# A fused attention, gated MLP and rational MLP in fp32: attention tiles of 64 queries by 96 keys with two heads on 128 partitions, in place of 96 by 128 of one head

## The chip, the cores and the metric

The kernel runs on one core of one Trainium2 chip. The metric is the device time of one launch in microseconds (us), as the median of several runs. Five engines work beside each other: TensorE (PE: matmuls and transposes; PEld is its loading of weights), VectorE (DVE), ScalarE (ACT), GpSimd (POOL) and SyncE (SP, which here issues the DMAs).

## The reference, cut to what matters

```python
def _attn_ref(q, k, v):                     # (4, 8, 576, 64) fp32
    window, dilation = 32, 4
    scores = (1.0 / np.sqrt(D)) * np.matmul(q, k.transpose(0, 1, 3, 2))
    rel = pos[:, None] - pos[None, :]
    mask_plain = (rel >= 0) & (rel < window)
    mask_dil = (rel >= 0) & (rel < window * dilation) & (rel % dilation == 0)
    masks = [mask_plain if h < H // 2 else mask_dil for h in range(H)]
    scores = np.where(masks[None], scores, -1e9)
    scores = scores - np.max(scores, axis=-1, keepdims=True)
    attn = np.exp(scores)
    attn = attn / (np.sum(attn, axis=-1, keepdims=True) + 1e-09)
    return np.matmul(attn, v)

x = attn_out.transpose(0, 2, 1, 3).reshape(2304, 512)
x = ((x @ w1) * (x @ w2) @ w3) @ w_out       # 512 -> 1024 -> 1024 -> 512
h = x @ w_in                                 # 512 -> 2048
P = a[0] + a[1] * h + a[2] * h * h + a[3] * h * h * h
Q = 1.0 + np.abs(b[0]) * np.abs(h) + np.abs(b[1]) * h * h
return (P / (Q + 1e-06)) @ moe2_w_out        # 2048 -> 512
```

The weights of the two MLPs arrive as fp64, and the kernel turns their words into fp32 itself.

## The kernel before

**Two phases.** `phase1` does the attention, the product of `w3` and `w_out` (so that the first MLP has one matrix less), the first MLP, and the decoding of all fp64 weights. `phase2` does the second MLP, `step(i)` by `step(i)`, with matmuls in `hmm` (L867) and `l4` (L917). The change doesn't touch `phase2`.

**Attention.** A unit `u` is one batch and one pair of heads (16 units), and a half unit `G` is half of its queries (32 of them). The queries of a dilated head are sorted by their position modulo 4, so that both masks become a band of 32 keys and a tile of queries needs one short piece of the keys. A tile is 96 queries by 128 keys, three tiles per head and half. The steps of a half unit are:

- Q, `att_qk` (L362): for each tile and head a matmul of K = 64, with the queries as weights (64 x 96) and 128 columns of keys moving. The two heads lie on partitions 0 to 63 and 64 to 127 and write to two banks of PSUM. An fp32 matmul is two records in the trace.
- `att_mask` (L382, DVE): adds the mask, scales, and takes the row's minimum; six per half. `att_exp` (L390, ACT): exponential and row sum; six per half. `att_sums` (L395, L397) and `att_norm` (L402), DVE.
- T, `att_pt` (L409): a transpose on PE for each tile and head, 96 x 128 of the probabilities as weights and 96 columns of the identity moving; three per head. `att_pc` (L415, ACT) copies the result out of PSUM.
- V, `att_pv` (L424): for each tile and head a matmul with 128 x 64 of the values as weights and 96 columns moving; the two heads write to partitions 0 to 63 and 64 to 127 of one bank.
- `att_high` (L464, ACT) and `att_low` (L468, DVE) split the result in a high and a low part for the MLP.

**The MLP and the weights.** `w3_mm` (L480) multiplies `w3` by `w_out`; `l1` (L501) and `l2` (L533) are the first MLP, 12 matmuls of 128 x 512 per output tile. `load` issues the DMA of a slab of weights; `scale` (L231) and `top_bits` (L262) on ACT and `ends` (L267) and `middle` (L271) on DVE decode it. The first slabs (`CUTS`) come in two pieces. `warm_up` (L318) fills PE with 11 matmuls before the first Q and 14 behind it.

**The order.** `phase1` makes a list of jobs, each with an engine, what it must come after and which buffers it takes, and `Plan.order` issues them in the order that the table `ORDER` gives, three hexadecimal digits a job. Each engine's queue then follows that order, and the waits between engines come from semaphores. `att_runs` groups Q and V: the first eight half units run one by one, later ones in pairs (V of two half units, then Q of the next two).

Of the kernel before, what the change touches and what calls it, by code (L numbers as in the profile page):

```python
# [41 lines left out]
QT = 96  # L42
# [20 lines left out]
CUT_W3 = (5, 6, 7)  # L63
BY_ACT1, BY_ACT2 = 0, 16
# [5 lines left out]
RUN_FROM = 8  # L70

# [12 lines left out]
def q_bank(g):  # L84
    return ("sc", "px")[g == 1 or g >= RUN_FROM and g % 2]


def t_bank(g):
    return ("px", "sc")[g >= RUN_FROM and g % 2 == 0]


def v_bank(g):
    return "sc" if g >= 30 else ("px", "acc")[g >= RUN_FROM]
# [6 lines left out]
    "1e70000011eb1f11e81e91f52001fb1ea1ef1ed1ec00300f0041f31f22051ee1f00061f71f60050101f41f81f91fa007"  # L100
    "20201120327c27b2010082042061fd1fc20701c52320a00201b20f1fe1ff21901227e00900a20820c21420b00b00d27d"
    "2b920d20e20901300c21100e22301401501701e21021e21b21221321a22a01802a21c21d21621523803a01f021217218"
    "02001622522422602b22703b23102221f22027f28028222c01d02302402524622b28122802601901a22122d22e02c027"
    "22222f22923a23902823f2c003c24d28423023b02d02e03802923323203d23c02f23423524825225705a05923d236030"
    "04903903e24903f24124704124004023703123e28328528628703203304a03403628824a24224303503724b04204304b"
    "24424c24525c2ab26125925804504624f24e28904404c04728a28b04828d04d25028c2512542532c228f29104f26605c"
    "28e25525625a25b27426d2932952972902c329205705805d25e2ad06826325d04e06925f05e050294296051264260053"
    "29805205529926726826926a2ac2620602652ae2af26f27005f06127626e05427127706329a2f82e32ce07e05b2d507f"
    "2b22dc2b005606a26b2722732752bb2ba06b06d07629b06229c26c06c06e2782b106429e07706f07107006629d2d62c1"
    "0650722c42bc2792d70672d82bd29f07307807427a2a02de2b42c50750792b307b2b52d92c62da2dd2a107a2b607c2b7"  # L110
    "2a22db07d2b82df30646330d2c70802ea0812f10b70990b609831409a2ff2a32a52a72a82a92be2aa08d08e2c82c92e5"
    "08f2ca31b0822bf2cb0832a42e031d09009109346409246508431c31e3210940962cc2cf2cd2a62d00852ec2e1086087"
    "0882e232332208908b32730830f0950972eb08a08c2e62d12d23242ed2ee2d32e42ef2fa2f33292d42e72f046646709b"
    "09c09d0b231f0f40d44694682e809e2f90b43102fb3280a732a2fc0b32e90a832d09f0a932f0a00a20b50aa0a132e333"
    "2f246a3003010ab0ac0ad46b3300ae0b00a30a50af3350b10a42fd0a63340b93022f43202f52f62fe46c3032f746d331"
    "32530730e3040d03360ba0c50c630930a30546e46f0d50b83390bc3163320bb33a33b30b0c70bd0c830c33c0be0c00d1"
    "0bf3110c933f34033d4703370ca0cb4713413120d20ce0c30c10cc3130d34724734753450cd0cf0c20c4315317318326"
    "31932b34231a3380d70d80ee0f00ef0f14763430da34747747847932c0d93460f21113480e333e0db0e53490dc3440dd"
    "0e40e634a0de0e70e834b34c34d34e3520ea0e10df0e90f30d647b47c47d47e47f47a1104814740ec0eb34f3530ed0e0"
    "0e23563503543553510f510110248248348448548012f48748610c1030f635735835910d10e1041051060f835a35d108"  # L120
    "0f710710a10f0f935b35e3614880fa0fc0fb35f0ff0fd48948a48b1090fe36310010b36211336411f11436012e36748d"
    "48e36935c48f49049149312a12112c11636812036a11512211736d36f36e37049449549649737337412312412511811a"
    "11911d12812611b37537612b12d37911c11e12736536637712937b36b49213011214c13149918937149a49b49c49d49f"
    "48c14d49e14837213213337a37c14914a13437f13513d13f38113e1401361381373804a03823781414a14a24a313b385"
    "38613938714314214b14414613a13c14538314738b38836c14f4a516c4a63894984a74a84a94ab18816b14e4a4166167"
    "37d16816938d38c15038e38f15215115b15c37e3841531544ac15e15d4ad4ae4af38a39015f1601551561614b14aa16a"
    "39139239339416216339539639715739816415816515939c15a39939a4b216d4b34b44b539d16e16f1841861791704b7"
    "1c539b1a64b618a17139e17a18717217318517417c17b1751764b817d17f17e39f1771781821803a31811834b94ba4bb"
    "18b3a03a43a13a54bd4b03a73a218c18d19719852418e3a94be3a83ad18f3aa3af1a21994bf4c04c11a81c43a64bc1a7"
    "4c31903ae3b01921913b31951933b419a19b19c19d3b11941963b51a419e3b23b61a51a31a03b919f1a14c43bb3b71a9"  # L130
    "4c54c64c74c91c01c23ba1b53b81b71b61c33bc1aa1ab1b83bf3c03c13bd1b93be3c24ca1ad4cb4cc4cd1ba1bb3c53c7"
    "3c63cb1ac1ae1af1bc1b11be4cf1b03cd3ab3ac1c13c81b33cc1bd1bf1b21b41c73c94d03ce4d14d24d33ca1c81de3c3"
    "1e01c64d54c84ce1df1e11ca3d13d33d21c93d43c41d33d53cf1d43d63d04d61d51d64d74d84d91d71d81cb1d91cc4db"
    "4da4c23d73d83d93da3de3e21da1ce1cd1dc1d11cf1db1dd1d01d23e34dc1e24dd4de4df1e31e54e11e41e63e43e53e6"
    "3e73e93ea3eb3e84d44e04e24e34e44e53ec4e73ed3ef3ee3df3f03f33f54e83f43e03f64e94ea4eb4ed3e14e63f73f1"
    "3f93fb3fa3fc3ff4014ee4ef4f04f14004023fd4033db3f23fe4044054064073dc3f84084f34f44f54f64f74f84f94f2"
    "40b40d40c40e41140f4094134124144fa4104fb4fc4fd4ff41741841940a5254fe52641a41b41541641c500501502503"
    "5054ec50650750850950b50450a3dd50c50d50e50f51141d41e41f42042142442842242542642742342942a42b42f433"
    "43443543643943b42c42d43a43c51242e51351451543043f44143d43e44044244544743751651751051851951a51b51d"
    "44644843144b44c43251c44944d44344443844e51e51f52052152252852e45145345245445745945845a45d45e45544f"  # L140
    "44a45052945f52a45b52f46046153046245645c52752b52c53153253352d"
# [45 lines left out]
class Kern:  # L187
# [91 lines left out]
    def high_g(self, s):  # L279
        s["w"] = self.gp.tile([P, 2, TB], F32R, tag="g", bufs=8, name="wg")  # L280
        self.nc.scalar.copy(s["w"][:, 0], s["x"])
# [10 lines left out]
    def consts(self, pool):  # L292
        nc = self.nc

        nc.scalar.preload_act_table_set("natural_log_exp_and_others")
        self.ident = pool.tile([P, P], F32, name="ident")
        nc.gpsimd.memset(self.ident, 0.0)
        nc.gpsimd.affine_select(out=self.ident, in_=self.ident, compare_op=ALU.not_equal,
                                fill=1.0, base=0, pattern=[[-1, P]], channel_multiplier=1)

        self.masks = pool.tile([QT, 3, P], F32, name="masks")
        nc.gpsimd.memset(self.masks, 0.0)
        for i in range(3):
            mk = self.masks[:, i]
            nc.gpsimd.affine_select(out=mk, in_=mk, compare_op=ALU.is_gt, fill=NEG, base=0,
                                    pattern=[[1, P]], channel_multiplier=-1)
            nc.gpsimd.affine_select(out=mk, in_=mk, compare_op=ALU.is_ge, fill=NEG, base=WIN,
                                    pattern=[[-1, P]], channel_multiplier=1)
        nc.gpsimd.memset(self.masks[:, 0, 0:WIN], NEG)
        mk = self.masks[:, 1, 0:80]  # L310
        nc.gpsimd.affine_select(out=mk, in_=mk, compare_op=ALU.is_gt, fill=NEG, base=48,
                                pattern=[[0, 80]], channel_multiplier=-1)
# [36 lines left out]
    def att_load_v(self, u):  # L349
        b, hp = divmod(u, HP)  # L350
        self.vb[u] = self.at.tile([P, 2, NTILE, D], F32, tag="vb", bufs=2, name="vb")
# [18 lines left out]
    def att_mask(self, G, h):  # L370
# [4 lines left out]
        if h == 0:  # L375
            self.pr[G] = at.tile([QT, 6, P], F32, tag="pr", bufs=3, name="pr")
            self.sm[G] = at.tile([QT, 3, 6], F32, tag="sm", bufs=4, name="sm")
        pr, sm = self.pr[G], self.sm[G]
        for t in range(3):
            mk = t if dil else (0 if half == 0 and t == 0 else 2)  # L380
            i = h * 3 + t
            nc.vector.tensor_tensor_reduce(  # L382
                out=pr[:, i], in0=self.sc[G][h][0:QT, t * P:(t + 1) * P], in1=self.masks[:, mk],
# [3 lines left out]
    def att_exp(self, G, h):  # L387
        pr, sm = self.pr[G], self.sm[G]
        for i in range(3 * h, 3 * h + 3):
# [711 lines left out]
```

## Time and profile before

| | |
|---|---|
| median of three runs | 824.01 us (823.68, 824.01, 827.56) |
| the profiled execution, its own time | 824.62 us |
| its span, first to last instruction | 822.8 us |
| PE busy | 814.1 us, 99% |
| PEld, DVE, ACT, POOL busy | 81%, 73%, 67%, 27% |
| the chain that ended last | PE 96%, DMA 2%, ACT 1%, DVE 1% |

The profile is of one execution. Busy time counts an engine's instructions; ends of matmuls are modelled, so that a matmul's duration overlaps the next one, and what a block of matmuls costs is read from its start to the start of the next block. L12 is line 12 of the kernel before. A row of the timeline gives start, length, engine, line, output and inputs, weights and moving shape, and the count; behind it in brackets the idle time before it.

### The profile page before, as it was taken

The page shows a single profiled execution, that of the slowest core. Times are in us where ns is not written, and L with a number is a line of the kernel's source. Part 1 is how long each engine was busy: PE and PEld are TensorE (multiplying, and loading weights), DVE is VectorE, ACT ScalarE, POOL GpSimd, SP SyncE. Part 2 cuts the span into 40 slices and gives each one's busy share as a digit, 9 for nine tenths or more (in the row PEclk, how much of TensorE's full clock was granted, in tenths as well). Part 3 has the DMA queues.
Part 4 walks back from the last instruction along what each step waited for, and adds up shares of the span by engine and source line. Part 5 has one row for each costly group of instructions (what it writes and reads, how often), then busy time and mean ns, then how long its engine had stood idle before and what let it go on. Part 6 is the DMA issues. An engine that isn't in the chain of part 4 may idle for free.

```text
span 822.8 us, 12622 instructions
## 1 busy us (share of the span) xinstructions
PE 814.1 (99%) x4426; PEld 668.8 (81%) x4426; DVE 602.7 (73%) x1325; ACT 547.5 (67%) x1223; POOL 225.2 (27%) x185
## 2 busy tenths in 40 slices
PE   8999999999999999999999999999999999999998
PEld 5556888888889988888888888888888888888886
DVE  6999999647777844325447888887789777797775
ACT  6999987555557632222438887777778777777773
POOL 1000000000000000000015655655547555465442
PEclk9999999999999999999999999999999999999999
DMA  8969434553456343544640000110001001001112
GB/s 302 363 229 362 137 120 135 167 183 108 145 192 204 105 146 115 192 141 140 235 136 25 27 14 14 28 37 14 14 14 38 27 14 25 2 25 53 51 52 77
DMA packets 38559, 90.74 MB, mean 110 GB/s; under 512 B 4192, under 2 KB 6240, under 8 KB 38496
## 3 DMA queue, kind: packets, MB, share of 16 engines
q1 hardware_dynamic: 38496, 89.93, 32.8%
q8 instruction: 35, 0.57, 0.3%
q14 instruction: 28, 0.23, 0.1%
HBM read 69.47 MB, written 20.45 MB: 109 GB/s over the span
## 4 chain that ended last, share of the span: by engine, by line
PE 96%; DMA 2%; ACT 1%; DVE 1%; issue 0%; SPq 0%; DVEq 0%
PE ab L501 24%; PE px L867 12%; PE ab L867 12%; PE acc L917 12%; PE sc L917 12%; PE acc L533 6%; PE ab L533 3%; PE sc L533 3%; PE acc L480 2%; PE ab L480 2%; PE sc L362 2%; PE acc L424 2%; PE px L409 1%; DMA words<-moe_w_out 1%; PE px L362 1%; PE sc L409 1%
## 5 line engine op out<-in xcount | busy, mean ns | idle before, releaser
L878 POOL TENSOR_TENSOR y<-y,v 128x512 f32<-128x512 f32 x72 | 96.4, 1339 | 551.9 <-DMA c<-wd 404.6
L501 PE MATMUL ab<-xs,w 128*128 128x512 f32 (+1 forms) x960 | 203.7, 371 | 0.2 <-DVE x2l L548 0.2
L501 PEld LDWEIGHTS ab<-xs,w 128*128 128x128 f32 x960 | 166.2, 189 | 31.0 <-DVE x2l L548 0.4
L917 PE MATMUL acc<-w,gg 128*128 128x512 f32 x432 | 109.1, 389 | 0.0
L917 PE MATMUL sc<-w,gg 128*128 128x512 f32 x432 | 108.9, 389 | 0.0
L867 PE MATMUL ab<-XS,w 128*128 128x512 f32 (+1 forms) x480 | 104.4, 368 | 0.0
L867 PE MATMUL px<-XS,w 128*128 128x512 f32 (+1 forms) x480 | 104.2, 368 | 0.0
L904 POOL TENSOR_TENSOR gg<-t,gg 128x512 fp32r<-128x512 f32 x72 | 94.1, 1307 | 10.8 <-ACT gg L903 10.1
L867 PEld LDWEIGHTS px<-XS,w 128*128 128x128 f32 x480 | 84.1, 188 | 15.3
L867 PEld LDWEIGHTS ab<-XS,w 128*128 128x128 f32 x480 | 84.1, 188 | 15.3
L917 PEld LDWEIGHTS acc<-w,gg 128*128 128x128 f32 x432 | 80.8, 188 | 16.6
L917 PEld LDWEIGHTS sc<-w,gg 128*128 128x128 f32 x432 | 80.8, 188 | 16.6
L390 ACT ACTIVATE pr<-pr,sm 96x128 f32<-96x128 f32 x192 | 74.9, 397 | 10.5 <-DVE sm L382 10.5
L895 DVE SCALAR_TENSOR_TENSOR v<-y,cs,r 128x512 f32<-128x512 f32 x72 | 71.0, 986 | 0.0
L231 ACT ACTIVATE dec<-words 128x512 f32<-128x512 f32 (+1 forms) x74 | 48.7, 665 | 27.9 <-DMA words<-moe_w_out 10.9
L513 DVE TENSOR_TENSOR p<-a_sb,ab 128x512 f32<-128x512 f32 (+1 forms) x40 | 25.3, 632 | 55.2 <-PE ab L501 38.3
L508 ACT COPY a_sb<-ab 128x512 f32<-128x512 f32 (+1 forms) x40 | 21.8, 546 | 61.2 <-PE ab L501 61.1
L887 ACT ACTIVATE r<-y,cs 128x512 f32<-128x512 f32 x72 | 52.1, 724 | 13.1 <-POOL y L878 12.8
L877 ACT ACTIVATE y<-v,cs 128x512 f32<-128x512 f32 x72 | 58.8, 817 | 2.4
L903 ACT CAST gg<-t 128x512 fp32r<-128x512 f32 x72 | 44.3, 615 | 15.1 <-DVE t L897 15.1
L533 PE MATMUL acc<-pp,w 128*128 128x512 f32 (+1 forms) x240 | 50.4, 368 | 0.0
L533 PEld LDWEIGHTS acc<-pp,w 128*128 128x128 f32 x240 | 41.8, 189 | 7.4
(107 smaller groups left out, 1241.2 us busy)
## 6 DMA issues: line engine op xcount, KB each, us to landing
words<-moe_w SPq DMA_DIRECT2D x31, 512.0 KB, 5.9
words<-moe_w_out SPq DMA_DIRECT2D x23, 512.0 KB, 4.2
words<-moe_w_in SPq DMA_DIRECT2D x16, 512.0 KB, 4.1
wd<-dec SPq DMA_DIRECT2D x32, 256.0 KB, 4.5
c<-wd SPq DMA_DIRECT2D x32, 256.0 KB, 2.7
vb<-v SPq DMA_DIRECT2D x16, 384.0 KB, 5.8
XS<-x2d SPq DMA_DIRECT2D x6, 1024.0 KB, 7.4
kT<-k SPq DMA_DIRECT2D x16, 304.0 KB, 4.8
```

The lines of the kernel that those rows point to most:

```text
L231: self.nc.scalar.activation(out=d.bitcast(F32), in_=s["words"].bitcast(F32)[:, :, 1], func=AF.Copy, scale=2.0 ** -112)
L390: self.nc.scalar.activation(out=pr[:, i], in_=pr[:, i], func=AF.Exp, scale=-1.0, bias=sm[:, 0, i:i + 1], accum_out=sm[:, 1, i:i + 1])
L501: self.nc.tensor.matmul(t[:, 0:nt], w[:, s[0], c * P:(c + 1) * P], xs[:, s[1], c], start=n == 0, stop=n == 11)
L533: self.nc.tensor.matmul(self.l2_acc[k, n][:, 0:nt], self.W3o[m][0][:, a, n * P:(n + 1) * P], self.p2[k, m][:, c, 0:nt], start=m == 0 and ( ...
L867: nc.tensor.matmul(t[:, e * nt:(e + 1) * nt], w[:, s[0], c * P:(c + 1) * P], XS[blk][:, s[1], c], start=n == 0, stop=n == 11)
L877: nc.scalar.activation(out=w, in_=v, func=AF.Identity, scale=self.b1, bias=self.b0)
L878: nc.gpsimd.tensor_tensor(out=w, in0=w, in1=v, op=ALU.mult)
L887: nc.scalar.activation(out=r, in_=yy[i][1], func=AF.Ln, bias=self.c1)
L895: nc.vector.scalar_tensor_tensor(out=v, in0=w, scalar=self.c1, in1=r, op0=ALU.add, op1=ALU.mult)
L903: nc.scalar.copy(t[:, 0], u)
L904: nc.gpsimd.tensor_tensor(out=t[:, 1], in0=u, in1=t[:, 0].bitcast(F32), op=ALU.subtract)
L917: nc.tensor.matmul(acc[g, blk][tk], t[:, s[0], j:j + P], w[:, s[1]], start=f + e == 0 and s == (0, 0), stop=f + e == FG - 1 and s == (1, 0))
```

## The change

It cuts the attention into nine tiles of 64 queries by 96 keys per unit (five in the first half, four in the second). The two heads of a pair stand on top of each other, on partitions 0 to 63 and 64 to 127, so that one mask, one exponential and one normalisation serve both. Q writes both heads to one bank (64 columns of weights each, 96 columns moving), T takes 64 x 96 of the probabilities with 64 columns of the identity moving and writes the heads to two banks, V has 96 x 64 as weights and 64 columns moving, of which the tile that lies across the middle is done in two parts of 32. The masks become six tiles of their own. T of a half unit is one job, no longer one per head. `ORDER` is another table.

```diff
-QT = 96
+QT = 64
+KW = 96
+TILES = ((0, 1, 2, 3, 4), (5, 6, 7, 8))
+PARTS = ((slice(0, 3), slice(3, 5)), (slice(0, 2), slice(2, 4)))
...
-    "1e70000011eb1f11e81e91f52001fb1ea1ef1ed1ec00300f0041f31f22051ee1f00061f71f60050101f41f81f91fa007"
+    "1c71cb1d10001d50011e01c91c81d31cd1d21cc1db1d71d61e501a1ca1d41cf1d91ce1d000300e1d81da1e20041ea1e1"
...
 def att_qk(self, G):
-        sc = self.sc[G] = [self.bank(q_bank(G)) for _ in range(2)]
-        for t in range(3):
-            j = (3 * half + t) * QT
+        sc = self.sc[G] = self.bank("sc")
+        for i, t in enumerate(TILES[half]):
             for h in range(2):
-                self.nc.tensor.matmul(sc[h][0:QT, t * P:(t + 1) * P],
-                                      qT[h * D:(h + 1) * D, j:j + QT],
-                                      kT[h * D:(h + 1) * D, j:j + P], start=True, stop=True)
+                r = slice(h * D, (h + 1) * D)
+                self.nc.tensor.matmul(sc[r, i * KW:(i + 1) * KW], qT[r, t * QT:(t + 1) * QT],
+                                      kT[r, t * QT:t * QT + KW], start=True, stop=True)
...
 def att_exp(self, G, h):
-        for i in range(3 * h, 3 * h + 3):
+        for i in range(5)[PARTS[G % 2][h]]:
...
-    def att_pt(self, G, h):
+    def att_pt(self, G):
-        pt = self.pt[G, h] = self.bank(t_bank(G))
-        for t in range(3):
-            self.nc.tensor.transpose(pt[:, t * QT:(t + 1) * QT], self.pr[G][:, h * 3 + t],
-                                     self.ident[0:QT, 0:QT])
+        pt = self.pt[G] = [self.bank("px") for _ in range(2)]
+        for i in range(len(TILES[G % 2])):
+            for h in range(2):
+                r = slice(h * QT, (h + 1) * QT)
+                self.nc.tensor.transpose(pt[h][0:KW, i * QT:(i + 1) * QT], self.pr[G][r, i], self.ident[r, r])
...
 def att_pv(self, G):
-        for t in range(3):
+        todo = ([(t, G, t, 0, QT if t < 4 else QT // 2) for t in range(5)] if half == 0 else
+                [(4, G - 1, 4, QT // 2, QT)] + [(t, G, t - 5, 0, QT) for t in range(5, 9)])
+        for t, g, i, a, b in todo:
+            at = t * QT + a - half * HS
             for h in range(2):
-                self.nc.tensor.matmul(xt[h * D:(h + 1) * D, t * QT:(t + 1) * QT],
-                                      vt[:, h, 3 * half + t], pT[:, h * 3 + t], start=True, stop=True)
+                self.nc.tensor.matmul(xt[h * D:(h + 1) * D, at:at + b - a],
+                                      vt[:, h, t], self.pT[g][:, h, i, a:b], start=True, stop=True)
```

The queue of PE where the pairs of half units have begun (`sc<-kT,qT` is Q, `px<-ident,pr` is T, `acc<-pT,vb` is V, `ab<-xs,w` is `l1`; the count is of matmuls, two trace records each for Q and V). Before:

```order
L362 MATMUL px<-kT,qT 96x128 x6
L501 MATMUL ab<-xs,w 128x512 x48
L409 MATMUL px<-ident,pr 128x96 x6
L409 MATMUL sc<-ident,pr 128x96 x6
L501 MATMUL ab<-xs,w 128x512 x12
L424 MATMUL acc<-pT,vb 64x96 x12
L362 MATMUL sc<-kT,qT 96x128 x6
```

and now:

```order
L366 MATMUL sc<-kT,qT 64x96 x18
L509 MATMUL ab<-xs,w 128x512 x36
L413 MATMUL px<-ident,pr 96x64 x8
L509 MATMUL ab<-xs,w 128x512 x12
L413 MATMUL px<-ident,pr 96x64 x10
L509 MATMUL ab<-xs,w 128x512 x12
L432 MATMUL acc<-pT,vb 64x64 x8
L432 MATMUL acc<-pT,vb 64x32 x4
L432 MATMUL acc<-pT,vb 64x64 x8
```

Twelve such rounds follow each other. Before, the transposes of the two half units stood together in six of the rounds and in two pieces in the other six; now they are in two pieces in all twelve, with `l1` or `l2` on both sides of each. Over the whole of phase 1, T is in 31 blocks before and in 32 now, and Q in 19 both times.

The queue of SP at the start of the program (`words` are weights, 256 KB where the shape is 128x512; `qT` 288 KB, `kT` 304 KB). Before:

```order
L213 DMA words<-moe_w_out 128x512
L342 DMA qT<-q 128x576
L347 DMA kT<-k 128x608
L213 DMA words<-moe_w_out 128x512
L213 DMA words<-moe_w 128x512 x2
```

and now:

```order
L209 DMA words<-moe_w_out 128x512 x2
L209 DMA words<-moe_w 128x512
L346 DMA qT<-q 128x576
L209 DMA words<-moe_w 128x512
L351 DMA kT<-k 128x608
```

The keys of the first unit were the third transfer and are now the sixth; the same six transfers come first both times. The queue of PE behind it still begins with 11 filler matmuls, the first Q (now 18 matmuls, before 12) and 14 filler matmuls.

## Rows read from the trace of the kernel before

**Rows 1.** The page, part 1: busy time, share of the span, instructions.

```profile
PE 814.1 (99%) x4426; PEld 668.8 (81%) x4426; DVE 602.7 (73%) x1325; ACT 547.5 (67%) x1223; POOL 225.2 (27%) x185
```

**Rows 2.** Windows: stretch, its length, then PE, PEld, DVE, ACT, POOL busy.

```profile
38.00:83.50 45.50, 45.49 (x264) 28.93 (x263) 44.42 (x128) 43.87 (x126) 0.00 (x0) 1.00 0.79 292
83.50:295.00 211.50, 211.31 (x1562) 181.06 (x1560) 164.48 (x583) 139.90 (x489) 0.00 (x0) 1.00 0.48 151
```

**Rows 3.** PE's waits, from the view of waits: total us, times, longest.

```profile
PE px L409 <- DVE pr L402: 1.7, 1, 1.7
...
PE px L424 <- ACT pT L415: 0.7, 1, 0.7
```

**Rows 4.** Timeline of PE, 91 to 114 us: one round and a half.

```profile
91.80 0.66 PE L409 MATMUL px<-ident,pr 96*128 96x96 f32 x6
92.24 3.00 PE L501 MATMUL ab<-xs,w 128*128 128x512 f32 x12
95.08 0.66 PE L409 MATMUL sc<-ident,pr 96*128 96x96 f32 x6
95.52 2.99 PE L501 MATMUL ab<-xs,w 128*128 128x512 f32 x12
98.44 1.21 PE L424 MATMUL acc<-pT,vb 128*64 128x96 f32 x24
99.58 0.90 PE L362 MATMUL sc<-kT,qT 64*96 64x128 f32 x12
100.31 0.82 PE L362 MATMUL px<-kT,qT 64*96 64x128 f32 x12
101.06 11.20 PE L501 MATMUL ab<-xs,w 128*128 128x512 f32 x48
112.09 0.66 PE L409 MATMUL px<-ident,pr 96*128 96x96 f32 x6
...
113.03 3.01 PE L501 MATMUL ab<-xs,w 128*128 128x512 f32 x12
```

**Rows 5.** Timeline of PE, 44 to 48.3 us, where half units run one by one.

```profile
44.61 0.72 PE L424 MATMUL px<-pT,vb 128*64 128x96 f32 x12
45.26 0.90 PE L362 MATMUL sc<-kT,qT 64*96 64x128 f32 x12
46.09 0.47 PE L409 MATMUL px<-ident,pr 96*128 96x96 f32 x3
...
48.09 0.41 PE L409 MATMUL px<-ident,pr 96*128 96x96 f32 x3
48.28 1.65 PE L480 MATMUL ab<-wg 128*128 128x512 f32 x6
```

**Rows 6.** Timeline of PE, 294 to 340 us: one long block and the next.

```profile
295.08 43.82 PE L501 MATMUL ab<-xs,w 128*128 128x512 f32 x192 [0.20 <-DVE x2l L548]
338.74 1.52 PE L533 MATMUL acc<-pp,w 128*128 128x512 f32 x6
```

**Rows 7.** Groups by form, PEld: weights' shape, count, busy us, mean ns.

```profile
L362 PEld LDWEIGHTS sc<-kT,qT 64*96 64x96 f32 x228 | 13.2, 159 | 3.0 <-issue 1.0
...
L424 PEld LDWEIGHTS acc<-pT,vb 128*64 128x64 f32 x264 | 11.3, 137 | 3.4 <-issue 2.1 <-ACT x L543 0.4 <-ACT dec L231 0.4
```

**Rows 8.** Timeline of PE and of SP's queue, first 12 us.

```profile
1.37 4.40 PE L318 MATMUL px<-ident 128*128 128x128 f32 x22 [1.37 <-POOL ident L298]
6.24 0.90 PE L362 MATMUL sc<-kT,qT 64*96 64x128 f32 x12 [0.47 <-DMA kT<-k]
...
7.73 3.39 PE L318 MATMUL ab<-ident 128*128 128x128 f32 x28
11.51 1.98 PE L480 MATMUL ab<-x 128*128 128x512 f32 x4 [0.39 <-DVE x L271]
...
2.59 1.38 SPq L213 DMA_DIRECT2D words<-moe_w  x3
```

**Rows 9.** DMA issues in the first 30 us: count, KB each, us to landing.

```profile
words<-moe_w SPq DMA_DIRECT2D x2, 256.0 KB, 5.0
```

More of the change, by code (lines that the diff above doesn't have):

```diff
@@ L63 @@
 CUT_W3 = (5, 6, 7)
+OHOME = {}
 BY_ACT1, BY_ACT2 = 0, 16
@@ L70 @@
 RUN_FROM = 8
+NPR, NPT = 3, 2
 def att_runs(n):
@@ L142 @@
+    "43f50950a44044151243543c51350750e50b44243650c50f42f51043050d"
 )
@@ L375, in att_mask @@
         if h == 0:
-            self.pr[G] = at.tile([QT, 6, P], F32, tag="pr", bufs=3, name="pr")
-            self.sm[G] = at.tile([QT, 3, 6], F32, tag="sm", bufs=4, name="sm")
+            self.pr[G] = at.tile([P, 5, KW], F32, tag="pr", bufs=NPR, name="pr")
+            self.sm[G] = at.tile([P, 3, 5], F32, tag="sm", bufs=4, name="sm")
         pr, sm = self.pr[G], self.sm[G]
-        for t in range(3):
-            mk = t if dil else (0 if half == 0 and t == 0 else 2)
-            i = h * 3 + t
+        for i in range(5)[PARTS[half][h]]:
+            t = TILES[half][i]
+            mk = 0 if t == 0 else {2: 2, 4: 3, 6: 4, 7: 5}.get(t, 1) if dil else 1
             nc.vector.tensor_tensor_reduce(
-                out=pr[:, i], in0=self.sc[G][h][0:QT, t * P:(t + 1) * P], in1=self.masks[:, mk],
+                out=pr[:, i], in0=self.sc[G][:, i * KW:(i + 1) * KW], in1=self.masks[mk],
                 op0=ALU.add, op1=ALU.min, scale=-0.125, scalar=3.0e38,
@@ L597, in phase1 @@
                                  add("SP", self.att_load_v, u, new=lb[2:3]), lb)
-                    sc = [buf(q_bank(G)) for _ in range(2)]
+                    sc = [buf("sc")]
                     after += [asked.get(G - 1), *ld[u][0:2]]
@@ L608, in phase1 @@
                     use += [pTb, ld[u][3][2]]
+                    if half:
+                        use.append(odd[G - 1][0])
+                        after += odd.pop(G - 1)[1]
+                    else:
+                        odd[G] = pTb, pcs
                     ps.append((G, xt))
@@ L611, in phase1 @@
             asked.update((G, run) for G, _ in qs)
-            for G, _ in ps:
-                done[G] = run
-                for j in pts.get(G + 2, ()):
-                    j.after.append(run)
             for G, sc in qs:
                 prb, smb, pTb = buf("pr"), buf("sm"), buf("pT")
-                m0 = add("DVE", self.att_mask, G, 0, after=[run], new=[prb, smb], use=sc[0:1])
-                m1 = add("DVE", self.att_mask, G, 1, after=[run, m0], use=[prb, smb, sc[1]])
+                m0 = add("DVE", self.att_mask, G, 0, after=[run], new=[prb, smb], use=sc)
+                m1 = add("DVE", self.att_mask, G, 1, after=[run, m0], use=[prb, smb] + sc)
                 es = [add("ACT", self.att_exp, G, h, after=[m], use=[prb, smb]) for h, m in enumerate((m0, m1))]
@@ L622, in phase1 @@
                 no = [add("DVE", self.att_norm, G, h, after=[su], use=[prb, smb]) for h in range(2)]
+                pb = [buf("px") for _ in range(2)]
+                pt = add("PE", self.att_pt, G, after=no, new=pb, use=[prb])
                 pcs = []
                 for h in range(2):
-                    pb = buf(t_bank(G))
-                    pt = add("PE", self.att_pt, G, h, after=[no[h], done.get(G - 2)], new=[pb], use=[prb])
-                    pts.setdefault(G, []).append(pt)
                     pcs.append(add("ACT", self.att_pc, G, h, after=[pt] + pcs,
-                                   new=[pTb] if h == 0 else [], use=[pb] + ([pTb] if h else [])))
+                                   new=[pTb] if h == 0 else [], use=pb[h:h + 1] + ([pTb] if h else [])))
                 out[G] = pTb, pcs
@@ L688, in phase1 @@
                 a = add("DVE", fn, s, after=a, use=[db, wb])
-                xbs[g, j] = buf("g")
+                if g == "o" and j in OHOME:
+                    s["slot"] = OHOME[j]
+                xbs[g, j] = buf(s.get("slot", "g"))
                 a = add("ACT", self.high_g, s, after=[a], new=[xbs[g, j]], use=[db])
@@ L1061, in lay_out @@
     vo = np.concatenate([np.zeros((B, H, WIN, D), v.dtype), order(v)], axis=2)
-    vw = np.stack([vo[:, :, t * QT:t * QT + P] for t in range(NTILE)], axis=2)
-    vw = vw.reshape(B, HP, 2, NTILE, P, D).transpose(0, 1, 4, 2, 3, 5).reshape(B, HP, P, -1)
+    vw = np.stack([vo[:, :, t * QT:t * QT + KW] for t in range(NTILE)], axis=2)
+    vw = vw.reshape(B, HP, 2, NTILE, KW, D).transpose(0, 1, 4, 2, 3, 5).reshape(B, HP, KW, -1)
     def words(x):
```

145 lines of the change are left out of this document (73 added, 72 removed).

## The prediction

> **What bounds the kernel now.** I read the busy times first: PE is busy for 814.1 of 822.8 us [rows 1]. The windows say where this could be loose, since phase 1 before 83.5 us also has DVE and ACT nearly full (44.42 and 43.87 of 45.50 us), but PE is busy there for 45.49 us, and for 211.31 of 211.50 us in the rest of phase 1 [rows 2]. The view of waits then lists what PE waited for: past the program's first microseconds the longest are 1.7 and 0.7 us [rows 3], and as the windows leave next to nothing behind 38 us, both lie ahead of it. So the time is the sum of PE's blocks and of a slow start. Relief for DVE and ACT can only give back these waits. What counts is what a block of Q, T or V costs on PE, and for that I go to the timeline of PE and read from the start of a block to the start of the next.
>
> **Prices of PE's blocks today.** Plain `l1` runs at (338.74 - 295.08) / 192 = 0.227 us a record [rows 6].
> - V: 12 records take 45.26 - 44.61 = 0.65 us [rows 5], 24 take 99.58 - 98.44 = 1.14 us [rows 4]. The two heads run beside each other, so I count pairs: six more cost 0.49, 0.082 us each, and 0.65 - 6 x 0.082 = 0.16 us is fixed.
> - Q: 12 records take 46.09 - 45.26 = 0.83 us [rows 5], 24 take 101.06 - 99.58 = 1.48 us [rows 4]: 0.108 us a pair and 0.18 us fixed.
> - V moves 96 columns and Q 128, so a column costs (0.108 - 0.082) / 32 = 0.0008 us. A pair of 96 columns is 0.082, one of 64 is 0.056, one of 32 would be 0.030.
> - T: six take 92.24 - 91.80 = 0.44 us, twelve 113.03 - 112.09 = 0.94 us [rows 4], 0.08 us each, with nothing fixed; they run one by one.
> - Around the blocks: twelve `l1` between T and T take 95.08 - 92.24 = 2.84 us, 0.11 more than 12 x 0.227, the loss on coming back from T. Between T and V they take 98.44 - 95.52 = 2.92 us, so that entering V costs 0.08 more. After Q, 48 take 112.09 - 101.06 = 11.03 us, 0.13 too much; I use 0.12 for coming back from either.
>
> So Q and V, which use a part of the array, pay about 0.17 us in themselves and 0.08 on entry. T with 96 x 128 weights pays neither.
>
> **The change on PE, in the twelve rounds of pairs.**
> - Q: 18 pairs of 96 columns instead of 12 of 128: 18 x 0.082 + 0.165 = 1.64 us against 1.48. 12 x 0.16 = **+1.9 us**. The weights are narrower (64 columns), and their load was already shorter than the movement.
> - V: 16 pairs of 64 columns and 4 of 32. The small ones lie between 0.030 by columns and the 0.056 of the others if the load of their weights, 64 columns as well, binds: loads of 96 and 64 columns take 159 and 137 ns [rows 7], 0.7 ns a column or 0.045 for 64. I take 0.04, nearest to that: 16 x 0.056 + 4 x 0.04 + 0.16 = 1.21 us against 1.14, 12 x 0.07 = **+0.9 us** (0.5 less or 0.8 more at the ends).
> - T: the open price. Its tile is now 64 rows and 96 columns of weights, for which today's rows have no transpose. The nearest rows are Q, whose weights are 64 x 96 too [rows 5], and T itself. I take the shape to decide: pairs side by side, and Q's fixed cost. A block of five pairs is 5 x 0.056 + 0.165 + 0.08 + 0.12 = 0.645 us, one of four 0.59 us, together 1.235 us a round. Today a round has one block of twelve (0.94 + 0.11 = 1.05) six times and two blocks (0.55 each, 1.10) six times. 12 x 1.235 - 6 x 1.05 - 6 x 1.10 = **+1.9 us**.
>
> The rule against this change is in the Trainium skill, TensorEngine Tiling (Array Packing), Key Properties: changing the tiling mode, not merely the tile, drains the engine. By that rule T pays like Q, and the sum is mine; by today's T rows alone it is that of rival 1. The trace agrees with the rule on Q and V, 0.16 and 0.18 us fixed, and no row shows it on T. The same page's Instruction Overhead says that a matmul of one column lasts as long as one of 60; by that a piece of 32 columns is an estimated 0.052 us, 0.6 us more in the twelve rounds.
>
> **The first eight half units.** Q: the first has 18 for 12 (+0.16), then three of 10 (0.98) and three of 8 (0.82) for six at 0.83: +0.6 in all. V: six at 8 x 0.056 + 2 x 0.04 + 0.16 = 0.69 for 0.65, +0.2. T: three blocks of six (0.55) and ten of three (0.19 + 0.11 = 0.30 [rows 5]), 4.65 us, become eight blocks, 4.9 us; two of these stand next to Q or V and save a return each, so +0.05. The `w3` product is broken up 14 times and no longer 17, 3 x 0.12 saved. Together **+0.5 us**.
>
> **The start.** Today Q starts at 6.24 us, held by the keys' transfer, fillers follow at 7.73, and the first `w3` matmul starts at 11.51 [rows 8]. The keys are now the sixth transfer, behind the same bytes that today's sixth has ahead of it. The first two of the three issues at 2.59 us, 0.46 us apart [rows 8], are 256 KB and land after 5.0 us [rows 9], so the sixth lands at 2.59 + 0.46 + 5.0 = 8.05 us. Q at 8.2, 1.64 us of Q, fillers of 3.39 us: `w3` begins at 13.2 us, **+1.7 us**; its first data, now fetched earlier, are ready by then. In return the waits of 1.7 and 0.7 us [rows 3] should go, since PE asks 1.7 us later for the first transposes and has 8 `w3` matmuls ahead of them where it had 6, with less attention work in front of them on DVE: **-2.4 us**. What is late next is the copy of T on ACT ahead of each V, 0.7 us once today. I leave **+0.5 us** for that (0 to 1.5). PE now idles from about 5.7 to 8.2 us. The longest idle time that today's trace has once PE is running is the 1.7 us of rows 3. If the granted clock fell from 2.4 to 1.2 GHz there, the start would be paid again: the first 22 filler records take 4.40 us where 28 later ones take 3.39 [rows 8], 4.40 - 22 x 0.121 = 1.7 us. I put that in the range.
>
> **At nothing.** Per unit masks and exponentials fall from 12 to 9, and DVE and ACT get faster; PE's own work covers both [rows 2]. If that cover went, it would be worth the waits above. The six masks in place of three are POOL's only work in phase 1, and it has until 8.2 us for the two that come first. The values' transfers are 442 KB for 393, on queues that no PE wait in the rounds names.
>
> **Sum.** 1.9 + 0.9 + 1.9 + 0.5 + 1.7 - 2.4 + 0.5 = +5.0 us on the profiled execution's 824.62 us. That stands 0.6 us above the median of 824.01, so I predict **829.0 us** as the median. What a measurement of this kernel can tell from no change is about 0.5%, 4.1 us: 819.9 to 828.1.
>
> **Rivals.**
> 1. *Transposes pair up and pay no entry, drain or first pair.* For it: T's own rows today show nothing fixed. Against: every block that uses part of the array does. A round's T costs 9 x 0.056 + 2 x 0.11 = 0.725 and not 1.235 us; over 16 units that is -8.2, **820.8 us**, not slower. It decides as soon as a block of T pays under 0.01 us of the 0.165, with entry still there; then the sum is at zero (32 blocks x 0.155 = 5.0).
> 2. *The two heads' transposes run one after the other*, as T's do today, and still switch. Against: Q's heads, of the same weights' shape, run in pairs. 9 more transposes of 0.056 a unit, 16 units: +8.1, **837 us**. Here the change wouldn't do on PE what two heads on 128 partitions promise.
> 3. *The new order earns more in the first 83 us than I see*: the keys land earlier (third transfer today, 6.1 us), and small waits inside the `w3` blocks vanish. That takes off 1.7 and up to some 3 us more: **824 to 826 us**. For it: DVE and ACT lose a quarter of their attention work where they are full. Against: PE has only the 2.4 us of waits to give there.
>
> **How the numbers follow.** The forecast has 0.58; its own range is 826 to 832.5, from the ends of the V pieces, the copies' wait and the clock. Rival 1 has 0.18, rival 2 0.12, rival 3 0.12. Slower by over 0.5%: two thirds of the forecast (0.37) and rival 2, 0.49. Within 0.5%: the rest of the forecast (0.21), rival 3, and 0.07 of rival 1, 0.40. Faster: 0.11, the part of rival 1 in which the start also gains a microsecond. The range to hold 8 in 10 reaches from the middle of rival 1 to the middle of rival 2: 820 to 837.
>
> **What would show it.** Right: in a round, T's blocks of ten and eight run in pairs with `l1` resuming over 0.2 us late; V and Q blocks of 1.2 and 1.64 us; the first Q at about 8.2 us; DVE and ACT less busy at no gain. Wrong: `l1` follows T within 0.03 us as today, or T's 18 records in a round take over 1 us without their entry and return, or PE waits in the rounds for masks or copies. A round that costs no more than today's would refute the forecast.

## The result, and the profile after

The changed kernel takes 830.88 us (median of 7 runs, 828.76 to 832.27), the kernel before 824.57 on the same chip (7 runs, 823.68 to 827.56): a ratio of 1.0071, interval 1.0052 to 1.0090. (The ratios here go by all runs and lie close to those of the means; the medians alone give 1.0077.) Forecast were 829.0 us and a range of 820 to 837. The profiled execution of the changed kernel took 829.05 us with a span of 827.3. That is 4.4 us more than the 824.62 of the kernel before; the sum had said +5.0. The medians lie 6.3 us apart. So most of the change is as forecast, and the changed kernel's median lies 1.8 us above its profiled execution, which has to be explained too.

The page's busy times, against [rows 1]: DVE is busy for 26 us less, ACT for 21 us less, and PE for 5.5 us more.

```profile
PE 819.6 (99%) x4970; PEld 668.6 (81%) x4970; DVE 576.3 (70%) x1229; ACT 526.7 (64%) x1127; POOL 226.9 (27%) x194
```

The windows, against [rows 2] (stretch, length, then busy time of PE, PEld, DVE, ACT, POOL, the granted clock, DMA share, GB/s): PE has no idle time left from 38 to 295 us, so the relief of DVE, 44.42 to 41.13 us in the first stretch, shortens nothing.

```profile
38.00:83.50 45.50, 45.50 (x347) 29.48 (x347) 41.13 (x108) 43.60 (x113) 0.00 (x0) 1.00 0.95 327
83.50:295.00 211.50, 211.50 (x1921) 175.69 (x1920) 138.98 (x500) 119.65 (x409) 0.00 (x0) 1.00 0.46 148
```

PE's waits, against [rows 3]: the 1.7 us for the first transposes and the 0.7 us for the copy are gone. In their place stand 1.8 us for the keys and 0.4 us for the values.

```profile
PE sc L366 <- DMA kT<-k: 1.8, 1, 1.8
PE px L322 <- POOL ident L295: 1.4, 1, 1.4
PE sc L432 <- DMA vb<-v: 0.4, 1, 0.4
PE ab L509 <- DVE x2l L556: 0.2, 1, 0.2
```

The timeline of PE at the start, against [rows 8], and the first V of all:

```profile
1.36 5.06 PE L322 MATMUL px<-ident 128*128 128x128 f32 x22 [1.36 <-POOL ident L295]
8.24 1.70 PE L366 MATMUL sc<-kT,qT 64*64 64x96 f32 x36 [1.82 <-DMA kT<-k]
9.87 3.39 PE L322 MATMUL ab<-ident 128*128 128x128 f32 x28
13.10 1.88 PE L488 MATMUL acc<-x 128*128 128x512 f32 x4
...
23.25 0.78 PE L432 MATMUL sc<-pT,vb 96*64 96x64 f32 x20 [0.43 <-DMA vb<-v]
```

The first Q starts at 8.24 us (8.2 forecast) and `w3` at 13.10 (13.2 forecast). And one round, with the start of the next, against [rows 4]:

```profile
82.97 8.48 PE L509 MATMUL ab<-xs,w 128*128 128x512 f32 x36
91.38 0.43 PE L413 MATMUL px<-ident,pr 64*96 64x64 f32 x8
91.74 3.01 PE L509 MATMUL ab<-xs,w 128*128 128x512 f32 x12
94.68 0.48 PE L413 MATMUL px<-ident,pr 64*96 64x64 f32 x10
95.10 3.01 PE L509 MATMUL ab<-xs,w 128*128 128x512 f32 x12
98.04 1.39 PE L432 MATMUL acc<-pT,vb 96*64 96x64 f32 x40
99.36 1.70 PE L366 MATMUL sc<-kT,qT 64*64 64x96 f32 x36
100.99 8.50 PE L509 MATMUL ab<-xs,w 128*128 128x512 f32 x36
109.42 0.43 PE L413 MATMUL px<-ident,pr 64*96 64x64 f32 x8
```

Read from start to start: Q 100.99 - 99.36 = 1.63 us, V 99.36 - 98.04 = 1.32 us, T 0.42 us for five pairs and 0.36 for four. The twelve `l1` between T and T take 2.94 us, 0.22 more than 12 x 0.227 [rows 6], where they took 2.84 [rows 4].

**Where the time went.** The first `l1` starts at 82.97 us, 0.53 us sooner than before. What follows it takes 827.3 - 82.97 = 744.3 us against 822.8 - 83.50 = 739.3, +5.0 us. For that stretch I added up PE's records by kind (from the trace, since the view merges them), each from its start to the start of the next record:

| from the first `l1` on, us | before | after | difference |
|---|---|---|---|
| Q | 16.32 | 17.96 | +1.64 |
| V | 13.69 | 15.79 | +2.10 |
| T | 11.36 | 9.26 | -2.10 |
| `l1` and `l2` | 300.90 | 304.26 | +3.36 |

`l1` and `l2` do the same work in both. They can differ by what they lose on entry to a block and on coming back from it, which is why T and they are read together: +1.26 us. T alone looks like a gain, and the loss stands in the rows of its neighbours. Phase 2 doesn't differ.

### The profile page after: what moved, and what is told of

It reads as the page before. It is cut to its first block, busy times and chain, and to the rows that moved or that the text cites. A ratio compares the mean times of both kernels' runs of the same rounds, so it can differ in the third digit from the quotient of the medians.

```text
span 827.3 us, 13521 instructions
## 1 busy us (share of the span) xinstructions
PE 819.6 (99%) x4970; PEld 668.6 (81%) x4970; DVE 576.3 (70%) x1229; ACT 526.7 (64%) x1127; POOL 226.9 (27%) x194
## 4 chain that ended last, share of the span: by engine, by line
PE 97%; DMA 2%; DVE 1%; SPq 0%; ACT 0%; issue 0%; DVEq 0%
PE ab L509 25%; PE ab L877 12%; PE px L877 12%; PE sc L927 12%; PE acc L927 12%; PE acc L541 6%; PE ab L541 3%; PE sc L366 3%; PE ab L488 3%; PE acc L488 3%; PE sc L541 3%; PE acc L432 2%; PE px L413 1%; DMA vb<-v 1%; PE sc L432 1%; DMA words<-moe_w 1%
## 5 line engine op out<-in xcount | busy, mean ns | idle before, releaser
L393 ACT ACTIVATE pr<-pr,sm 128x96 f32<-128x96 f32 x144 | 52.3, 368 | 15.1 <-DVE sm L385 14.9
```

What stands on the lines that cost most here:

```text
L393: self.nc.scalar.activation(out=pr[:, i], in_=pr[:, i], func=AF.Exp, scale=-1.0, bias=sm[:, 0, i:i + 1], accum_out=sm[:, 1, i:i + 1])
```

## The experiments

My theory: T, with a tile of 64 rows, now drains PE as Q and V do; V's pieces of 32 columns cost more than I took; and the median's surplus over the profiled execution comes from the first microseconds. Rivals: T's price comes from the number of its matmuls; the surplus comes from the order of the first transfers. Ratios are to the kernel before on the same chip in the same hour. Its own median there was 825.69, 824.71 and 823.87 us in the three groups of runs, so ratios of one group compare best.

### T as one full transpose of both heads

```diff
-            for h in range(2):
-                r = slice(h * QT, (h + 1) * QT)
-                self.nc.tensor.transpose(pt[h][0:KW, i * QT:(i + 1) * QT], self.pr[G][r, i], self.ident[r, r])
+            b, c = divmod(i, 3)
+            self.nc.tensor.transpose(pt[b][0:KW, c * P:(c + 1) * P], self.pr[G][:, i], self.ident)
```

`att_pc` then copies three tiles of both heads from the one bank and the rest from the other.

> Edit to the changed kernel: one transpose takes both heads at once, 128 rows of weights by 96 columns with 128 columns of the identity moving, so that T no longer uses half of the array's rows. Theory (T's gain by pairs is eaten by the change of shape on entry and return): a block of five costs 5 x 0.109 less the 0.05 us that follows early, and the next matmuls lose 0.11 us as after T in the kernel before; about 0.58 us for five and 0.47 for four against 0.63 and 0.58 now, so 0.16 us a unit less, 2.5 us in all: about 828.3 us against 830.9 of the changed kernel. Rival (pairs are worth what they stream, the shape costs nothing): 9 x (0.109 - 0.056) = 0.48 us a unit more, 7.6 us: about 838 us.

Measured: 828.58 us, ratio 1.0034 (1.0022 to 1.0046). The timeline of PE in a round:

```profile
84.34 8.47 PE L509 MATMUL ab<-xs,w 128*128 128x512 f32 x36
92.66 0.60 PE L412 MATMUL px<-ident,pr 128*96 128x128 f32 x4
93.01 3.02 PE L509 MATMUL ab<-xs,w 128*128 128x512 f32 x12
95.87 0.71 PE L412 MATMUL px<-ident,pr 128*96 128x128 f32 x5
96.33 3.01 PE L509 MATMUL ab<-xs,w 128*128 128x512 f32 x12
99.27 1.39 PE L432 MATMUL acc<-pT,vb 96*64 96x64 f32 x40
```

Five transposes take 0.46 us, a little more than the five pairs. But the `l1` ahead of each block of T are shorter: 36 take 92.66 - 84.34 = 8.32 us for 8.41, twelve 95.87 - 93.01 = 2.86 for 2.94. Behind T next to nothing changes: the twelve from T to V take 2.94 us in both, and 0.02 us more on the average of the rounds. From the first `l1` on the kernel takes 826.8 - 84.34 = 742.5 us, 1.8 less than the changed kernel; T with `l1` and `l2` comes to 311.62 us there against 313.52, and 312.26 before. (In this profiled execution the first `l1` came 1.4 us late; its granted clock was 0.50 from 10 to 12 us, which the last experiments take up.) So the theory holds for T: what costs is that it is tiled. The edit also halves the number of T's matmuls, but the loss stands ahead of T, where none of them has run, and it is the same ahead of eight and of ten, 0.22 us with the return from the block before. This is the rule of the Trainium skill, TensorEngine Tiling (Array Packing), Key Properties, that a change of the tiling mode drains the engine. The trace agrees: on the average of the twelve rounds `l1` and `l2` lose 0.08 us more ahead of a tiled block of eight than ahead of a full one, and 0.11 us more ahead of one of ten.

### The keys as the third transfer

```diff
-    "1c71cb1d10001d50011e01c91c81d31cd1d21cc1db1d71d61e501a1ca1d41cf1d91ce1d000300e1d81da1e20041ea1e1"
+    "1c70000011cb1d11d51e01c91c81d31cd1d21cc1db1d71d61e501a1ca1d41cf1d91ce1d000300e1d81da1e20041ea1e1"
```

(001 is the keys' transfer, 000 the queries', 1c7 to 1e0 are weights.)

> Edit to the changed kernel: in the order's table the first unit's queries and keys are loaded second and third, as in the kernel before, the rest unchanged. Theory (the later keys cost 1.7 us of PE at the start, and the idle time ahead of Q lets the granted clock fall in some executions): first Q at 6.2 us, first w3 matmul at about 11.2 us instead of 13.1, 828 to 829 us and a narrow spread. Rival (the start is bound by the transfers of weights and values anyway): w3 starts earlier, PE then waits about 1.7 us longer for the values before the first V, and the time stays at 829 to 831 us, but for the clock.

Measured: 830.27 us, ratio 1.0065 (1.0046 to 1.0083), 828.73 to 833.21. The timeline of PE:

```profile
6.35 1.73 PE L366 MATMUL sc<-kT,qT 64*64 64x96 f32 x36
8.01 3.39 PE L322 MATMUL ab<-ident 128*128 128x128 f32 x28
11.24 1.88 PE L488 MATMUL acc<-x 128*128 128x512 f32 x4
...
23.23 0.78 PE L432 MATMUL sc<-pT,vb 96*64 96x64 f32 x20 [1.60 <-DMA vb<-v]
```

Q starts 1.9 us earlier and `w3` too, and then PE waits for the values until 23.23 us, where it stood at 23.25 in the changed kernel. The first `l1` comes at 83.00 us, not sooner. The rival holds: what PE gains by early keys it waits for at the values. Two of the six runs have a mean granted clock of 0.995 and 0.996 (the share of its full clock that PE was allowed) and took 833.06 and 833.21 us, though in the profiled execution PE doesn't idle before Q; where the clock fell in those two, no profile shows.

### Longer fillers ahead of Q

```diff
-WARM = 11, 14
+WARM = 19, 14
```

> Edit to the changed kernel: 19 fillers ahead of the first Q instead of 11, so that PE has no idle time until the keys land at 8.2 us; all else, the keys' place too, as in the changed kernel. Theory (the changed kernel's spread of 828.8 to 832.3 us comes from the clock that falls in the idle time ahead of the first Q): all runs within 1 us of each other near 829.0, a granted clock of 0.998 to 0.999. Rival (the spread has another cause): median 830.5 to 831 with the same spread.

Measured: 830.50 us, ratio 1.0063 (1.0051 to 1.0075), 830.39 to 831.59. The runs lie closer together, as the theory has it, and all have a mean granted clock of 0.999 to 1.000, but they don't lie lower. In its profiled execution the keys landed later (Q at 9.10 us), `l1` began at 83.62, and PE waited 0.8 us for `x2l` at L556 where the changed kernel waits 0.2. On its own this run settles nothing; the last pair of experiments takes it up.

### The keys third and the values seventh

```diff
-    "1c71cb1d10001d50011e01c91c81d31cd1d21cc1db1d71d61e501a1ca1d41cf1d91ce1d000300e1d81da1e20041ea1e1"
...
+    "1c70000011cb1d11d50021e01c91c81d31cd1d21cc1db1d71d61e501a1ca1d41cf1d91ce1d000300e1d81da1e20041ea"
...
```

(002 is the values' transfer, which leaves its later place in the next line.)

> Edit to the changed kernel: queries and keys of the first unit second and third, and its values loaded seventh instead of behind thirteen other transfers. Theory (with keys and values early PE's start is bound by decoding alone): first w3 matmul at 11.2 us, no wait before the first V, 827 to 828 us, 1 to 1.7 us below the kernel that moves the keys alone. Rival (weights that land a microsecond later hold w3 up as much): no faster than the kernel that moves the keys alone.

Measured: 830.98 us, ratio 1.0070 (1.0057 to 1.0083). PE now waits for decoded weights, whose transfers stand behind the values:

```profile
5.76 1.70 PE L366 MATMUL sc<-kT,qT 64*64 64x96 f32 x36 [0.27 <-DMA kT<-k]
7.39 3.39 PE L322 MATMUL ab<-ident 128*128 128x128 f32 x28
10.62 1.94 PE L488 MATMUL acc<-x 128*128 128x512 f32 x4
12.39 1.88 PE L488 MATMUL ab<-x 128*128 128x512 f32 x4
16.80 0.70 PE L488 MATMUL ab<-x 128*128 128x512 f32 x1 [2.52 <-DVE x L267]
```

The first `l1` comes at 84.84 us. Part of that is the clock, which was granted at 0.50 from 18 to 20 us and 0.65 from 20 to 22, behind the wait of 2.5 us. In both orders tried, another transfer is late instead, and neither is clearly faster than the changed kernel's. In the changed kernel the DMA engines' busy share is 1.00 or more in every stretch of 2 us from 4 to 24 us, so the likely bound of the start is the bytes; no run with fewer of them shows it.

### V cut at 320 queries

The first half unit holds the five tiles of 64 queries whole and the second the other four, so that no tile lies across the border; `att_x` (which splits V's result for the MLP) and `touched` follow.

```diff
-        todo = ([(t, G, t, 0, QT if t < 4 else QT // 2) for t in range(5)] if half == 0 else
-                [(4, G - 1, 4, QT // 2, QT)] + [(t, G, t - 5, 0, QT) for t in range(5, 9)])
+        for i, t in enumerate(TILES[half]):
...
-                t0 = b * S + half * HS
-                lo, hi = max(at, t0), min(at + n, t0 + HS)
+                t0 = b * S + half * 320
+                lo, hi = max(at, t0), min(at + n, t0 + (320, 256)[half])
```

> The first half unit holds 320 queries and the second 256, so that no tile of V lies across the border: 18 pairs of 64 columns in a pair of half units in place of 16 of 64 and 4 of 32. ACT and DVE get one more small piece of the split for each dilated half unit and chunk. Theory: a pair of 32 columns lasts nearly as long as one of 64 (0.052 to 0.058 us), because the load of its weights, not its columns, sets the pace. Then V's block in a round falls from 1.315 to 1.20 us, and with 16 units the kernel loses 1.7 to 1.9 us: ratio to before 1.0050 where the changed kernel has 1.0071. Rival 1 (a pair of 32 columns costs 0.040 us and V is slow for another reason): the block falls to 1.235 us at most and would still be over the 18 x 0.056 + 0.16 = 1.17 us of the prediction's prices; 1.2 to 1.3 us gained. Rival 2: the additional pieces on ACT and DVE delay the first MLP in the first 83 us, so that the first l1 comes later than 82.97 us and the gain is lost.

Measured: 829.83 us, ratio 1.0062 (1.0047 to 1.0076). The timeline of PE:

```profile
84.74 8.48 PE L516 MATMUL ab<-xs,w 128*128 128x512 f32 x36
...
99.81 1.27 PE L429 MATMUL acc<-pT,vb 96*64 96x64 f32 x36
101.00 1.70 PE L366 MATMUL sc<-kT,qT 64*64 64x96 f32 x36
```

The block falls from 1.32 to 1.19 us with two pairs fewer, and from the first `l1` (84.74 us) on the kernel takes 743.0 us for 744.3. V over the whole program falls from 21.41 to 19.63 us: in each of 16 units four pairs of 32 columns gave way to two of 64, and 1.78 / 16 = 0.111 us went. With 0.056 for a pair of 64, one of 32 costs (0.111 + 2 x 0.056) / 4 = 0.056 us. The price of the theory holds: a piece of 32 columns costs what one of 64 does. The records of the changed kernel say so directly: inside a block of V the pairs start 0.058 us apart, those of 64 columns and, on average, those of 32. Whether the load of its weights or a shortest duration of a matmul is behind that, this run doesn't tell. The Trainium skill, TensorEngine Tiling (Array Packing), Instruction Overhead, says that a matmul of one column lasts as long as one of 60. The 0.056 us agree with it roughly (0.052 was the estimate from it).

The ratio gave 0.7 us where 1.7 to 1.9 were expected. In the profiled execution PE idled 2.5 us before Q, and the granted clock was 0.56 and 0.58 in the stretches from 10 to 14 us: the first `l1` came 1.8 us later than in the changed kernel's profiled execution, and there that took the gain. The rival said that the additional pieces on ACT and DVE would delay the first `l1`. It falls by the kernels below, which have the same pieces and longer fillers: their first `l1` comes at 82.70 and 83.03 us. What kept the median up is less clear, since two of this kernel's three slowest runs had a mean clock of 1.000.

### The full transpose with longer fillers, and all three edits

The first of these is the first experiment with `WARM = 19, 14`; the second has V cut at 320 queries too.

> The kernel with one full transpose for both heads, and 19 fillers ahead of the first Q in place of 11, so that PE does not idle before the keys land. In the profiled execution of the full-transpose kernel PE idled 2.7 us there, the first Q ran at half pace (3.10 us for 1.70) and l1 began at 84.35 us. Theory (the idle time lets the clock fall, and the start is paid at half pace): Q takes 1.6 to 1.7 us, l1 begins at 83.0 to 83.5 us, the runs lie closer together and the median is 0.3 to 1 us below the ratio 1.0034 of the full-transpose kernel (1.0022 to 1.0031). Rival: the clock falls only in a few executions, the longer fillers push Q back as often as they help, and the median stays within 0.0005 of 1.0034.

> All three edits together: one full transpose of both heads, V cut at 320 queries, and 19 fillers ahead of the first Q. Theory: the costs add, 1.0034 less 1.8 us (0.0022) for V and less 0 to 1 us for the start: ratio 1.000 to 1.0013, so 825 to 826 us where the kernel before has 825; what is left over the kernel before is Q (+1.9 us in the rounds) and V (+0.7), against what T gains. Rival: the small matmuls are not the cause of the difference, and the ratio stays at 1.003 or more although V's block is shorter.

Measured for the first: 828.07 us, ratio 1.0040 (1.0026 to 1.0054), 826.71 to 829.63. Its profiled execution is as expected (Q 1.70 us, `l1` at 83.00), and all seven runs have a mean granted clock of 0.999 to 1.000 where six of the eight with short fillers had 0.997 or 0.998. But the ratio isn't lower than 1.0034 and the runs don't lie closer. So the clock falls in most runs with short fillers, against the rival, and the longer ones hold it; but the time that this was to bring doesn't show. 1.0040 is just outside the rival's 1.0034 within 0.0005, and a comparison across two groups of runs can't decide by so little.

Measured for all three edits: 825.80 us (825.35 to 827.25, 11 runs), ratio 1.0011 (1.0001 to 1.0020). This is the theory's number. It ran in the group of the border kernel without the other edits, and is 4.0 us below that one.

### Each of the two without the other

These separate T from the fillers, both with V cut at 320 queries.

> V cut at 320 queries and 19 fillers ahead of the first Q, with the changed kernel's transposes of one head each: the kernel of all three edits without the full transpose. Theory: the kernel of all three edits (ratio 1.0011) plus what T's change of tiling costs over full transposes (1.9 us, from the start of the first l1 on: 744.33 against 742.5 us), so ratio 1.0034; the clock does not fall at the start, since PE idles 1.4 us before Q and not 2.5. Rival: the longer fillers are worth nothing, and the ratio is that of the border kernel without them, 1.0050 to 1.0062.

> One full transpose of both heads and V cut at 320 queries, with 11 fillers ahead of the first Q as in the changed kernel: all three edits without the longer fillers. Theory: in most executions the clock falls while PE idles 2 us and more before the first Q, which costs about 1.4 us (first l1 at 84.3 to 84.7 in two such profiled executions, 82.7 to 83.0 in those without): ratio 1.0011 plus 0.7 to 1.7 us, 1.0020 to 1.0032, and a mean granted clock of 0.997 to 0.998 in most runs. Rival: the fall of the clock is made good later, before l1 begins, and the ratio is 1.0011 within 0.0006.

Measured: T tiled with longer fillers 827.85 us, ratio 1.0045 (1.0031 to 1.0058). Its number was to be 1.0034, the rival's 1.0050 to 1.0062; it lies between them, and the interval holds the one and most of the other, so the ratio decides nothing. Its mean clock was 0.999 to 1.000 in all five runs. From its first `l1` (83.03 us) on it takes 743.0 us against 740.9 with full transposes, 2.1 us, as expected.

The full transpose with short fillers: 826.86 us, ratio 1.0024 (1.0015 to 1.0034), the theory's number; the medians alone give 1.0036, above the theory's 1.0032 and further still from the rival's 1.0011. The nine runs tell more than their median: two with a mean granted clock of 1.000 and 0.999 took 824.87 and 825.46 us, seven with 0.997 or 0.998 took 826.32 to 827.00. The profiled execution is one of the seven. The timeline of PE, and then the windows (the granted clock is the third number from the end):

```profile
8.70 2.52 PE L366 MATMUL sc<-kT,qT 64*64 64x96 f32 x36 [2.42 <-DMA kT<-k]
11.15 4.17 PE L322 MATMUL ab<-ident 128*128 128x128 f32 x28
15.16 1.88 PE L495 MATMUL acc<-x 128*128 128x512 f32 x4
```

```profile
8.00:10.00 2.00, 1.30 (x25) 1.33 (x27) 0.85 (x2) 0.60 (x3) 0.00 (x0) 0.85 1.03 422
10.00:12.00 2.00, 2.00 (x20) 1.78 (x17) 1.80 (x8) 2.00 (x8) 0.00 (x0) 0.50 1.01 409
12.00:14.00 2.00, 2.00 (x16) 2.00 (x16) 1.90 (x15) 2.00 (x9) 0.00 (x0) 0.80 1.04 414
```

From 10 to 12 us the granted clock is 0.50, the level of 1.2 GHz, after PE had idled 2.42 us. With all three edits PE idled 1.39 us before Q and the clock stayed at 1.00:

```profile
8.85 1.70 PE L366 MATMUL sc<-kT,qT 64*64 64x96 f32 x36 [1.39 <-DMA kT<-k]
10.48 3.39 PE L322 MATMUL ab<-ident 128*128 128x128 f32 x28
13.71 1.88 PE L495 MATMUL acc<-x 128*128 128x512 f32 x4
```

```profile
10.00:12.00 2.00, 2.00 (x27) 1.88 (x23) 1.78 (x8) 1.98 (x7) 0.00 (x0) 1.00 1.03 417
```

The keys land within 0.2 us of each other in both, and `w3` starts 1.45 us later in the one whose clock fell. The first `l1` is 1.45 us later too (84.15 and 82.70 us), and from there on both take 740.9 us. So a fall costs 1.45 us here; among the nine runs of the one kernel the slow seven and the fast two lie 0.9 to 2.1 us apart.

That the fillers keep the fall away shows best in the count. Of the kernels that load the keys sixth, those with 11 fillers have a mean granted clock of 0.998 or less in 22 of 30 runs (the changed kernel 5 of 7, with full transposes 6 of 8, with the border 4 of 6, with both 7 of 9). Those with 19 have it in none of 28.

In the changed kernel's own seven runs the two with a mean clock of 0.999 took 828.76 and 829.05 us, and the five with 0.996 to 0.998 took 830.50 to 832.27. So the clock goes with the surplus of the median over the profiled execution, which was one of the two. That it is the cause isn't shown. With longer fillers alone the clock held in all five runs, and the median was still 830.50; its profile shows 0.6 us more at `x2l` and 0.65 at the start. And the border kernel's two runs at 1.000, with 830.18 and 830.35 us, are slower than three of its four at lower clocks. What delays those is open.

No version beats the kernel before. The best executions of the best two (824.87 and 825.35 us) stand over 823.5, the best of the kernel before.

## Why the prediction was right, point by point

- **What bounds the kernel.** Right. PE has no idle time from 38 to 295 us, and 47 us less work on DVE and ACT bought nothing there.
- **Q, +1.9 us in the rounds.** A block takes 1.63 us for 1.64 forecast. From the first `l1` on it is +1.64, in eleven of the twelve blocks.
- **V, +0.9 us.** This is the term that was mis-sized: it measured +2.1, beyond its own upper end of +1.7. The block was put at 1.21 us and takes 1.32. "I take 0.04" for a piece of 32 columns was the step that failed. The four cost 0.058 each, what the pairs of 64 do, and that is 0.07 of the 0.106 us. The step took it near the load time scaled by the columns of the weights, 0.045, and no row of before has such a short matmul. The rest is the pair of 64 itself, 0.058 where the price by columns was 0.056.
- **T, +1.9 us.** The mechanism is right: pairs side by side, with entry and return. A block of five was put at 0.645 us and takes 0.42 + 0.22 = 0.64; of four 0.59 for 0.58. Read over the whole stretch with `l1` and `l2` it is +1.26 and not +1.9. The records show where the difference lies. T's own blocks were put 0.03 us too high each (0.445 and 0.39 without entry and return, for 0.413 and 0.358), 0.75 us in 24 blocks. The sum took 0.94 us for each block of twelve transposes in the kernel before, and one of them took 1.35 (289.00 - 287.65), 0.41 more:

```profile
287.65 0.66 PE L409 MATMUL px<-ident,pr 96*128 96x96 f32 x6
288.38 0.84 PE L409 MATMUL sc<-ident,pr 96*128 96x96 f32 x6
289.00 1.67 PE L533 MATMUL ab<-pp,w 128*128 128x256 f32 x12
```

Against that `l1` and `l2` grew by 3.36 us, where entry and return in the sum come to 24 x 0.20 - 18 x 0.11 = 2.8. Full transposes instead make T with `l1` and `l2` 0.64 us cheaper than before.
- **Rival 1** (T pays no entry) falls: `l1` ahead of T loses 0.08 to 0.11 us that it doesn't lose ahead of a full transpose, and five pairs take 0.42 us, 0.14 more than 5 x 0.056. **Rival 2** (transposes one after the other) falls: five pairs in 0.42 us. **Rival 3** (the order earns more at the start) was right in part: the first `l1` comes 0.5 us sooner, where the terms of the first eight half units, the start and the waits gave +0.3. Most of that is in the first eight half units: without the waits, the stretch from the first `w3` to the first `l1` went from 69.59 to 69.44 us, -0.15 where the sum had +0.5.
- **The start.** Q at 8.24 and `w3` at 13.10 are as worked out, and both old waits went. What is late next is not T's copy on ACT, for which I left 0.5 us, but the transfer of the values, 0.4 us. The price was right for another cause.
- **The clock.** I priced the fall after PE's idle time at 1.7 us and put it "in the range". The row behind that price, the first 22 filler records, has a granted clock of 1.00 in the view, so it doesn't show the price of a fall; the later pair of traces gives 1.45 us. The fall belonged in the forecast: by their mean clock five of seven runs have it, and they are the five slow ones. Whether it makes the median 830.88 where the profiled execution has 829.05 is not settled, since the longer fillers alone kept the clock and the median stayed at 830.50.
- **Luck.** The sum missed the profiled execution by only 0.6 us because its errors cancel: V was put 1.2 us too low, and T 0.65, Q 0.3 and the start 0.8 too high (half of Q's is its twelfth block, which lies ahead of the first `l1`).

## What to carry to other kernels

A narrow matmul needn't get cheaper with its width: here 32 columns cost what 64 did. So cut a tile's border so that no small pieces arise, even if the halves become unequal. A short block of tiled operations makes its untiled neighbours pay, and the loss stands in their rows: read blocks from start to start, with the neighbours, and try the operation that uses the whole array. And where a change makes PE idle early in a program, look at each run's mean granted clock before believing one profiled execution.

## What the runs showed of the hardware that was not expected

- With the same 11 fillers the clock came out either way: 1.8 us of idle time at 6.4 to 8.2 us and a granted clock of 1.00 in the changed kernel's profiled execution, 2.4 to 2.7 us and 0.50 to 0.56 from 10 to 12 us in others. The kernel before has such executions too: in the last group, nine of its thirteen runs, at 1.000, took 823.52 to 824.49 us, and four at 0.998 took 824.92 to 826.09.
- The keys, sixth on their queue in all of these, let Q start at 8.2 to 9.1 us from one profiled execution to the next, and the 11 fillers ended at 5.9 to 6.4; the two together decide how long PE idles.
- Five full transposes of 128 x 96, each doing both heads of a tile, take 96.33 - 95.87 = 0.46 us, 0.092 each; five pairs of 64 x 96 take 0.42, 0.084 a pair. In blocks as short as these, two halves of the array beside each other do the same work hardly faster than one transpose that uses it whole, and pay the entry on top. But from four tiles to five a block of pairs grows by 0.055 us and one of full transposes by 0.11. With the 0.10 us more that `l1` and `l2` lose around a tiled block, an estimate from these rows puts the two even at about six tiles; beyond that pairs should win. No run here has such a block.
